# Moving two K copies from VectorE to ScalarE, and cutting an output scaling in two, in a fused attention and token-mixing kernel

## The chip, the cores and the metric

One core of one Trainium2 chip. The metric is the device time of one execution in microseconds (us). "Before" is the kernel before, "changed" is the kernel after the change.

One more measure is used throughout, because end-to-end times scatter by about half a microsecond: the **attention part**, from the start of the first logits matmul (qT by kT) to the end of the span, in the profiled run of each kernel. Both edits lie inside it. And "**lost**" is TensorE time between two matmul starts beyond what that pair of shapes usually takes from start to start in the kernel before.

## The reference, cut to what matters

```python
x = A_x;  xn = _layernorm(x)                       # 2048 x 1024
return x + _A_ref(xn, wq, wk, wv, wo, beta) + _B_ref(xn, w1, b1, w2, b2)
# _A_ref: 32 heads of 32, four segments of 512 rows; per segment s and head:
logits = einsum(qs, ks) * scale + causal_mask
a_dot  = softmax(logits) @ vs
a_mem  = (phi(qs) @ M) / (phi(qs) @ z + 1e-06)     # memory of the earlier segments
o      = g * a_mem + (1 - g) * a_dot
M, z   = M + phi(ks).T @ vs, z + sum(phi(ks))      # phi(t) = t + 1 where t > 0, else exp(t)
# _B_ref: layernorm, two matmuls over the token axis, gelu between (done before the attention part)
```

## The kernel before

The attention part works in 32 units (four heads of one segment each: unit = 8 * segment + group). TensorE's instruction stream is made by hand from three kinds of work: dense projections (q, k, v, output), logits, and the weighting of v by the probabilities. Four PSUM banks hold logits, two hold weighted sums, two hold projections, so a bank that is not evicted in time stops TensorE (the 0.319 us lost at 483.91 and 0.326 us at 503.18, in the table below, are such stops).

```python
def q_job(self, u):            # q of unit u, projected in unit u-2
    def end(b):
        fw.op("act", lambda e: e.activation(self.qT[k][:], self.bank(b), ACT.Copy), ...)

def k_job(self, u):            # K: only for u < 16; from unit 16 K is read from DRAM
    def end(b):
        fw.op("dve", lambda e: e.tensor_copy(self.kT[k][:], self.bank(b)), ...)

def logits(self, u, step):     # four or eight matmuls, then one exponential, then the causal masks
    ...
    fw.op("act", ... ACT.Exp ...)
    for v, kb, _ in blocks:
        fw.op("pool", lambda e: e.affine_select(d, d, ...), ...)

def weigh(self, u, part):      # parts 0, 1, 2; banks 4, 5, 4
    ...                        # reads the masked probabilities, writes bank b
    fw.op("dve", lambda e: e.tensor_tensor(dst, src, eps, op=ALU.add), ..., writes=[self.R_ost[o][part]])

def combine(self, u):          # runs on VectorE between the dense matmuls of the next unit
    def products():            # weighted sums times 1/denominator and gate, 128 x 1024
        fw.op("dve", lambda e: e.tensor_tensor(self.prod[:], ost[:, :, 0:D_HEAD],
              rec.unsqueeze(2).to_broadcast([P, 32, D_HEAD]), op=ALU.mult), ...)
    def add():                 # the memory half plus the softmax half -> o_s
        ...
    return [scales, products, add]

# in attention(), unit u:  logits(u,0) ... weigh(u-1,0), weigh(u-1,1), weigh(u-1,2) ... logits(u,1) ...
```

In the profile `ost` is the eviction of the weighted sums, `kT` the copy of K, `prod` the scaling, `o_s` the sum of both outputs, `fin` the eviction of the output projection, `pT` the exponential (ScalarE) or the mask (POOL, which is GpSimd).

Of the kernel before, what the change touches and what calls it, by code (L numbers as in the profile page):

```python
# [6 lines left out]
ACT = mybir.ActivationFunctionType  # L7
ALU = mybir.AluOpType
# [7 lines left out]
D_HEAD = 32  # L16
# [3 lines left out]
P = 128  # L20
# [366 lines left out]
class _Kernel:  # L387
# [862 lines left out]
    def q_job(self, u):  # L1250
# [5 lines left out]
                self.exps.append((0, self.qT[k], self.R_qT[k], u))  # L1256
        return self.proj_job(self.wq_ring, u, end)

    def k_job(self, u):
        def end(b):  # L1260
            fw, k = self.fw, u % 3
            fw.op("dve", lambda e: e.tensor_copy(self.kT[k][:], self.bank(b)),  # L1262
                  reads=[self.R_bank[b]], writes=[self.R_kT[k]])
            if u // N_GRP < N_SEG - 1:
                self.exps.append((1, self.kT[k], self.R_kT[k], u))
        return self.proj_job(self.wk_ring, u, end)
# [167 lines left out]
    def combine(self, u):  # L1434

        fw = self.fw
        s, g, o = u // N_GRP, u % N_GRP, u % 2
        ost, R_ost = self.ost[o], self.R_ost[o]
        rec, R_rec = self.srec[:, o, :], self.R_srec[o]
        os, R_os = self.o_s[o], self.R_os[o]  # L1440

        def scales_first():
            v = ost[:].rearrange("p (q k r) x -> p q k r x", q=4, k=2)
            rv = rec[:, 0:16].rearrange("p (q r) -> p q r", q=4)
            fw.op("dve", lambda e: e.reciprocal(rv, v[:, :, 0, :, D_HEAD]), reads=R_ost, writes=[R_rec])
            fw.op("dve", lambda e: e.tensor_tensor(rv, rv, self.gate[:, g, None, 0, :].to_broadcast([P, 4, 4]),
                                                   op=ALU.mult), reads=[R_rec, self.R_gate], writes=[R_rec])

        def products_first():
            v = ost[:].rearrange("p (q k r) x -> p q k r x", q=4, k=2)  # L1450
            rv = rec[:, 0:16].rearrange("p (q r) -> p q r", q=4)
            fw.op("dve", lambda e: e.tensor_tensor(os[:].rearrange("p q (r d) -> p q r d", d=D_HEAD),
                                                   v[:, :, 0, :, 0:D_HEAD],
                                                   rv.unsqueeze(3).to_broadcast([P, 4, 4, D_HEAD]), op=ALU.mult),
                  reads=R_ost + [R_rec], writes=[R_os])

        def scales():
            sums = ost[:, :, D_HEAD].rearrange("p (q a) -> p q a", q=4)
            rv = rec.rearrange("p (q a) -> p q a", q=4)
            g8 = self.gate[:, g, :, :].rearrange("p k r -> p (k r)")[:, None, :].to_broadcast([P, 4, 8])  # L1460
            fw.op("dve", lambda e: e.reciprocal(rv, sums), reads=R_ost, writes=[R_rec])
            fw.op("dve", lambda e: e.tensor_tensor(rv, rv, g8, op=ALU.mult), reads=[R_rec, self.R_gate], writes=[R_rec])

        def products():
            fw.op("dve", lambda e: e.tensor_tensor(self.prod[:], ost[:, :, 0:D_HEAD],  # L1465
                                                   rec.unsqueeze(2).to_broadcast([P, 32, D_HEAD]), op=ALU.mult),
                  reads=R_ost + [R_rec], writes=[self.R_prod])

        def add():
            pv = self.prod[:].rearrange("p (q k r) d -> p q k (r d)", q=4, k=2)  # L1470
            fw.op("dve", lambda e: e.tensor_tensor(os[:], pv[:, :, 0, :], pv[:, :, 1, :], op=ALU.add),
                  reads=[self.R_prod], writes=[R_os])

        if s == 0:
            return [scales_first, products_first]
        return [scales, products, add]

    def o_transpose_dma(self, u):
# [199 lines left out]
```

## Time and profile before

| | kernel before |
|---|---|
| median of six runs beside the change (lowest, highest) | 652.36 us (652.19, 652.78) |
| span of the profiled run | 650.55 us |
| TensorE / VectorE / ScalarE / GpSimd busy | 99% / 67% / 43% / 24% |
| first logits matmul, attention part | 387.50 us, 263.05 us |
| lost in front of a weighting, waiting for `ost` behind a K copy | 0.319 us at 483.91, 0.326 us at 503.18 |
| lost in front of a weighting, waiting for a mask | 0.154 us at 547.74, 0.154 us at 577.70 |

TensorE is the bound, and it is nearly full. A change that does not touch TensorE's work can win only what TensorE loses in waits. A matmul of 512 columns is recorded with 0.38 us although the next one starts 0.215 us after it, so recorded matmuls overlap; this is why the waits are taken from starts.

### The profile page before, as it was taken

What the parts mean: (1) busy time and instruction counts of PE and PEld (TensorE: products, weight loads), DVE (VectorE), ACT (ScalarE), POOL (GpSimd) and SP (SyncE); (2) the same over time, 40 slices, a digit from 0 to 9 for tenths busy, and PEclk for the clock granted to TensorE, in tenths of its full rate; (3) what the DMA queues carried; (4) which work ended last, traced back from release to release, by engine and by line L of the source; (5) the groups of instructions that cost most, each with busy time, mean ns of one, the idle gap of its engine ahead of it and who ended that gap; (6) DMA issues with size and microseconds to landing.
All of it is one profiled execution on the core that took longest, in us unless ns stands there. A gap on an engine that the chain in (4) does not pass through costs nothing.

```text
span 650.5 us, 11182 instructions
## 1 busy us (share of the span) xinstructions
PE 645.9 (99%) x4611; PEld 303.6 (47%) x4611; DVE 433.7 (67%) x808; ACT 281.4 (43%) x305; POOL 154.2 (24%) x179
## 2 busy tenths in 40 slices
PE   9999999999999999999999999999999999999998
PEld 3444444444444444444444444444544454445544
DVE  6975676665555664744638325767887888777896
ACT  7543232232210000111101047778767778889770
POOL 2500000000011220220202203343334444554440
PEclk9999999999999999999999999999999999999999
DMA  9804233242498947538262957979654677435434
GB/s 303 216 0 130 65 107 88 64 116 79 127 261 193 238 120 210 157 102 231 79 208 96 263 130 177 184 168 227 134 135 98 155 165 139 112 98 128 105 94 139
DMA packets 190123, 95.00 MB, mean 146 GB/s; under 512 B 108664, under 2 KB 176248, under 8 KB 190072
## 3 DMA queue, kind: packets, MB, share of 16 engines
q1 hardware_dynamic: 189928, 94.25, 57.2%
q8 instruction: 36, 0.59, 0.4%
q14 instruction: 15, 0.12, 0.1%
q10 hardware_dynamic: 144, 0.03, 0.0%
HBM read 69.23 MB, written 11.53 MB: 124 GB/s over the span
## 4 chain that ended last, share of the span: by engine, by line
PE 94%; DVE 3%; ACT 2%; issue 1%; DMA 0%; POOL 0%; DVEq 0%
PE ps_all L199 94%; ACT pT L1364 1%; DVE prod L1465 1%; DVE ln_st L587 1%; DMA xin<-in_A_x_dram 0%; DVE h L627 0%; DVE ost L1418 0%; POOL ln_rs L611 0%; DVE mtmp L1230 0%; DVE kT L1262 0%; DVE fin L1307 0%; DVE mtmp L1228 0%; ACT qT L1253 0%; ACT vA L1293 0%; DVE ln_mv L590 0%
## 5 line engine op out<-in xcount | busy, mean ns | idle before, releaser
L1364 ACT ACTIVATE pT<-ps_all 128x2048 bf16<-128x2048 f32 x80 | 150.2, 1877 | 47.4 <-PE ps_all L199 46.9
L1368 POOL TENSOR_SCALAR_AFFINE_SELECT pT<-pT 128x512 bf16<-128x512 bf16 x128 | 105.6, 843 | 160.7 <-ACT pT L1364 160.7
L689 DVE TENSOR_TENSOR part<-ps_all,part 128x512 f32<-128x512 f32 x84 | 57.7, 690 | 108.2 <-PE ps_all L199 87.8
L1075 POOL TENSOR_TENSOR part<-part,stg 128x512 f32<-128x512 f32 x24 | 33.0, 1404 | 285.1 <-DVE part L689 285.1
L199 PE MATMUL ps_all<-wv,xnT 128*128 128x512 bf16 x256 | 68.5, 380 | 0.4 <-ACT qT L1253 0.2
L746 ACT ACTIVATE g<-part,b1c 128x512 f16<-128x512 f32 x36 | 26.0, 722 | 98.8 <-DVE part L689 98.8
L199 PE MATMUL ps_all<-xnT,wq 128*128 128x512 bf16 x256 | 66.4, 380 | 0.0
L199 PE MATMUL ps_all<-wo,oT 128*128 128x512 bf16 (+2 forms) x272 | 63.8, 367 | 0.0
L694 ACT ACTIVATE part<-ps_all 128x512 f32<-128x512 f32 x24 | 14.0, 596 | 101.1 <-PE ps_all L199 67.1
L1418 DVE TENSOR_TENSOR ost<-ps_all,eps 128x396 bf16<-128x396 f32 (+1 forms) x72 | 37.2, 522 | 28.5 <-PE ps_all L199 27.8
L199 PEld LDWEIGHTS ps_all<-vA,pT 128*128 128x128 bf16 x1280 | 45.7, 96 | 20.4 <-DVE ost L1418 1.7
L199 PE MATMUL ps_all<-g,sum 128*128 128x512 f16 x224 | 51.0, 379 | 0.0
L199 PE MATMUL ps_all<-g,w2s 128*128 128x512 f16 x224 | 51.0, 379 | 0.0
L199 PE MATMUL ps_all<-gT,sum 128*128 128x512 f16 x224 | 50.3, 379 | 0.0
L199 PE MATMUL ps_all<-vA,pT 128*128 128x33 bf16 x1280 | 48.5, 177 | 0.3 <-DVE ost L1418 0.3
L199 PE MATMUL ps_all<-h,sum 128*128 128x512 f16 x192 | 45.2, 379 | 0.0
L199 PE MATMUL ps_all<-h,w1s 128*128 128x512 f16 x192 | 44.9, 379 | 0.0
L199 PE MATMUL ps_all<-hT,sum 128*128 128x512 f16 x192 | 43.6, 379 | 0.0
L199 PEld LDWEIGHTS ps_all<-wo,oT 128*128 128x128 bf16 x272 | 23.9, 98 | 24.4 <-issue 3.7
L199 PEld LDWEIGHTS ps_all<-xnT,wq 128*128 128x128 bf16 x256 | 22.6, 97 | 25.4 <-issue 5.3
L199 PEld LDWEIGHTS ps_all<-g,sum 128*128 128x128 f16 x224 | 21.9, 98 | 26.4
L199 PEld LDWEIGHTS ps_all<-g,w2s 128*128 128x128 bf16 x224 | 21.9, 98 | 26.4
(118 smaller groups left out, 875.1 us busy)
## 6 DMA issues: line engine op xcount, KB each, us to landing
w2s<-in_B_w_dram SPq DMA_DIRECT2D x8, 1792.0 KB, 9.5
w1s<-in_B_w_dram SPq DMA_DIRECT2D x12, 1024.0 KB, 5.6
wq<-in_A_wq_dram SPq DMA_DIRECT2D x32, 256.0 KB, 3.3
xs<-in_A_x_dram SPq DMA_DIRECT2D x24, 256.0 KB, 3.4
stg<-in_A_x_dram SPq DMA_DIRECT2D x16, 256.0 KB, 2.9
out_dram<-stg SPq DMA_DIRECT2D x16, 256.0 KB, 3.9
wk<-in_A_wk_dram SPq DMA_DIRECT2D x16, 256.0 KB, 3.6
fin<-out_dram SPq DMA_DIRECT2D x16, 256.0 KB, 3.2
```

What stands on the lines that cost most here:

```text
L199: ins = self.nc.tensor.matmul(*args, **kwargs)
L587: fw.op("dve", lambda e: e.bn_stats(st[:, 6 * h:6 * h + 6], src[:, 512 * h:512 * h + 512]), reads=[self.R_xin[c]], writes=[R])
L689: self.fw.op("dve", lambda e: e.tensor_tensor(self.tmp[dst][:], self.bank(b), self.tmp[src][:], op=ALU.add), reads=[self.R_bank[b], self.R ...
L694: self.fw.op("act", lambda e: e.activation(self.tmp[dst][:], self.bank(b), ACT.Copy), reads=[self.R_bank[b]], writes=[self.R_tmp[dst]])
L746: self.fw.op("act", lambda e: e.activation(self.gB[f % 2][half][:, f // 2, :], src, ACT.Gelu_apprx_tanh, bias=self.b1c[:, f:f + 1], scale= ...
L1075: fw.op("pool", lambda e: e.tensor_tensor(self.tmp[t][:], self.tmp[t][:], self.stg[k][:, 512 * half:512 * half + 512], op=ALU.add), reads= ...
L1364: fw.op("act", lambda e: e.activation(dst, src, ACT.Exp, scale=SCALE), reads=self.R_bank[0:4], writes=[R[v % 2][kb] for v, kb, _ in blocks ...
L1368: fw.op("pool", lambda e: e.affine_select(d, d, pattern=[[0, 4], [1, P]], compare_op=ALU.is_ge, fill=0.0, base=0, channel_multiplier=-1), ...
L1418: fw.op("dve", lambda e: e.tensor_tensor(dst, src, eps, op=ALU.add), reads=[self.R_bank[b], self.R_eps], writes=[self.R_ost[o][part]])
L1465: fw.op("dve", lambda e: e.tensor_tensor(self.prod[:], ost[:, :, 0:D_HEAD], rec.unsqueeze(2).to_broadcast([P, 32, D_HEAD]), op=ALU.mult), ...
```

## The change

Its intent: in two units the K copy stands in VectorE's queue right before the eviction that TensorE waits for, so it goes to ScalarE. And in later units the long scaling holds up a causal mask on GpSimd that TensorE waits for (the one at 546.09 takes 1.50 us where the median mask takes 0.637), so in seven of them it is cut in two, to let the mask in between.

```diff
+    K_BY_ACT = (13, 15)
     def k_job(self, u):
         def end(b):
-            fw.op("dve", lambda e: e.tensor_copy(self.kT[k][:], self.bank(b)), ...)
+            if u in self.K_BY_ACT:
+                fw.op("act", lambda e: e.activation(self.kT[k][:], self.bank(b), ACT.Copy), ...)
+            else:
+                fw.op("dve", lambda e: e.tensor_copy(self.kT[k][:], self.bank(b)), ...)
 ...
         def products():
-            fw.op("dve", lambda e: e.tensor_tensor(self.prod[:], ost[:, :, 0:D_HEAD], ...
+            parts = ((0, 16), (16, 32)) if u >= 18 and u % 2 == 0 else ((0, 32),)
+            for a0, a1 in parts:
+                fw.op("dve", lambda e: e.tensor_tensor(self.prod[:, a0:a1], ost[:, a0:a1, 0:D_HEAD], ...
```

More of the change, by code (lines that the diff above doesn't have):

```diff
@@ L1261, in end @@
             fw, k = self.fw, u % 3
-            fw.op("dve", lambda e: e.tensor_copy(self.kT[k][:], self.bank(b)),
-                  reads=[self.R_bank[b]], writes=[self.R_kT[k]])
+            if u in self.K_BY_ACT:
+                fw.op("act", lambda e: e.activation(self.kT[k][:], self.bank(b), ACT.Copy),
+                      reads=[self.R_bank[b]], writes=[self.R_kT[k]])
+            else:
+                fw.op("dve", lambda e: e.tensor_copy(self.kT[k][:], self.bank(b)),
+                      reads=[self.R_bank[b]], writes=[self.R_kT[k]])
             if u // N_GRP < N_SEG - 1:
@@ L1464, in products @@
         def products():
-            fw.op("dve", lambda e: e.tensor_tensor(self.prod[:], ost[:, :, 0:D_HEAD],
-                                                   rec.unsqueeze(2).to_broadcast([P, 32, D_HEAD]), op=ALU.mult),
-                  reads=R_ost + [R_rec], writes=[self.R_prod])
+            parts = ((0, 16), (16, 32)) if u >= 18 and u % 2 == 0 else ((0, 32),)
+            for a0, a1 in parts:
+                fw.op("dve", lambda e: e.tensor_tensor(self.prod[:, a0:a1], ost[:, a0:a1, 0:D_HEAD],
+                                                       rec[:, a0:a1].unsqueeze(2).to_broadcast([P, a1 - a0, D_HEAD]),
+                                                       op=ALU.mult), reads=R_ost + [R_rec], writes=[self.R_prod])
         def add():
```

## The prediction

> **What bounds the kernel now.** I began with the page: busy time by engine, then the chain of work that ended last.
>
> ```profile
> PE 645.9 (99%) x4611; PEld 303.6 (47%) x4611; DVE 433.7 (67%) x808; ACT 281.4 (43%) x305; POOL 154.2 (24%) x179
> PE 94%; DVE 3%; ACT 2%; issue 1%; DMA 0%; POOL 0%; DVEq 0%
> ```
>
> TensorE is busy for 99% of a 650.5 us span and makes 94% of the chain. Neither edited part touches TensorE's own work, so the change can only give back time in which TensorE waits for someone. The chain in order of time shows where, in the attention part:
>
> ```profile
> 482.09 0.69 DVE mtmp L1230
> 482.78 0.60 DVE kT L1262
> 483.38 0.49 DVE ost L1418
> 483.87 0.05 issue
> 483.91 11.86 PE ps_all L199 x127
> ...
> 502.05 0.60 DVE kT L1262
> 502.65 0.49 DVE ost L1418
> 503.14 0.05 issue
> 503.18 42.96 PE ps_all L199 x485
> ```
>
> Columns are start, length, what. Twice the chain leaves TensorE for a burst on VectorE that ends with the K copy out of PSUM (kT, L1262) and the eviction of the weighted sums (ost, L1418), for which TensorE waits. K for unit u is projected in unit u-2, and the 32 groups of 512-column logits number the units, so these two copies are K of units 13 and 15, exactly the pair that the change names. No later unit has one (from unit 16 K comes from DRAM), and the earlier ones are not on the chain.
>
> How long TensorE really stands still is not the bracketed idle time, because matmuls overlap and their ends are modelled. I use starts. Eight 512-column matmuls in a row show as 1.90 us while one shows 0.38, so the pitch is (1.90 - 0.38)/7 = 0.217 us (start to start 0.215).
>
> ```profile
> 483.17 0.59 PE L199 MATMUL ps_all<-wv,xnT 128*128 128x512 bf16 x2
> 483.91 0.24 PE L199 MATMUL ps_all<-vA,pT 128*128 128x33 bf16 x3 [0.16 <-DVE ost L1418]
> ...
> 502.00 1.02 PE L199 MATMUL ps_all<-wv,xnT 128*128 128x512 bf16 x4
> 503.18 0.29 PE L199 MATMUL ps_all<-vA,pT 128*128 128x33 bf16 x5 [0.16 <-DVE ost L1418]
> ```
>
> Two matmuls from 483.17 are through at 483.60, the next starts at 483.91: 0.31 us lost. Four from 502.00 are through at 502.86, the next starts at 503.18: 0.32 us lost.
>
> The second edit is for another wait, which the profile does not name. I found it by laying GpSimd's causal masks (affine select, L1368) beside VectorE's scaling (L1465):
>
> ```profile
> 545.88 1.22 DVE L1465 TENSOR_TENSOR prod<-ost,srec 128x1024 bf16<-128x1024 bf16 x1
> 546.09 1.50 POOL L1368 TENSOR_SCALAR_AFFINE_SELECT pT<-pT 128x512 bf16<-128x512 bf16 x1 [2.77 <-ACT pT L1364]
> 547.13 0.74 DVE L1471 TENSOR_TENSOR o_s<-prod 128x512 bf16<-128x512 bf16 x1
> ...
> 547.37 0.38 PE L199 MATMUL ps_all<-wv,xnT 128*128 128x512 bf16 x1
> 547.74 0.25 PE L199 MATMUL ps_all<-vA,pT 128*128 128x33 bf16 x4
> ```
>
> A mask takes 0.637 us (median of the 128); this one takes 1.50 and ends at 547.59, about 0.5 us after the scaling ends at 547.10. The next weighting needs that mask and starts 0.15 us later; TensorE could have started at 547.37 + 0.215 = 547.585, so 0.155 us is lost. The same picture recurs at 577.70 (0.145 lost). In the five other units concerned it isn't there: at 562.84 the mask is only just in time (0.01 lost), at 592, 607, 621 and 635 it ended well before.
>
> [...] The K copies here have a median of 690 ns and the scaling 1218[...]. [...] the q copies out of PSUM here take 592 to 603. [...] the q copies stand between exponentials and no load follows. [...] masks beside the scaling go from 0.637 to 1.5 us, the scaling itself from 1.218 to 1.655 where a mask came first, and each side gets its turn when one instruction of the other ends (o_s takes 0.740 instead of 0.417 at 547.13, +0.32).
>
> **The change part by part.**
>
> K to ScalarE. VectorE loses 2 x 0.69 us. In both bursts its ost eviction starts 0.60 earlier (the start-to-start step from the K copy): 482.70 instead of 483.30, ending 483.26; with the 0.05 us of issue TensorE may go at 483.31, before the 483.60 at which it is free. In the other unit, 502.52 + 0.05 against 502.86. The stalls go entirely, with some 0.29 us to spare: 0.31 + 0.32 = **0.63 us** gained. ScalarE gains 2 x 0.6 us. Its surroundings:
>
> ```profile
> 479.12 0.60 ACT L1253 ACTIVATE qT<-ps_all 128x512 bf16<-128x512 f32 x1
> 481.19 1.88 ACT L1364 ACTIVATE pT<-ps_all 128x2048 bf16<-128x2048 f32 x1 [1.47 <-PE ps_all L199]
> 485.60 1.88 ACT L1364 ACTIVATE pT<-ps_all 128x2048 bf16<-128x2048 f32 x1 [1.00 <-PE ps_all L199]
> ...
> 504.43 1.88 ACT L1364 ACTIVATE pT<-ps_all 128x2048 bf16<-128x2048 f32 x1 [0.57 <-PE ps_all L199]
> ```
>
> K's last matmul ends at 480.82 (478.93 + 1.89), so the copy runs from about 480.85 to 481.45 in the 1.47 us idle stretch. It pushes the exponential that was to start at 481.19 back by 0.2 us. Before the next exponential ScalarE idles 1.00 us, in the second unit 0.57; TensorE arriving 0.32 earlier and the 0.2 delay use up 0.52. It fits, the second time just barely. Nothing for it on the path.
>
> The scaling in halves. It acts in seven units (outputs 18, 20 ... 30). One half should take 692 ns, as the first segment's 512-element scaling does (691 to 692 undisturbed). The second waits for the first through the semaphore of the shared tile, starting 0.03 us after it as dependent neighbours do. Undisturbed the pair takes 0.69 + 0.03 + 0.69 = 1.41 us, 0.19 more than 1.22. In return the mask gets its turn at half time: first half 545.88 to 546.57, mask through at about 547.07 instead of 547.59, in time for TensorE. But the mask's turn now falls into the second half (+0.32, as it did into o_s), and the second mask's turn still falls into o_s. VectorE is then behind by 0.19 + 0.32 = 0.5 us: ost would end at 548.95 + 0.51 = 549.46 and free TensorE at 549.51. Without the first stall TensorE wants that bank at 549.60 - 0.155 = 549.445. About 0.07 of the gain is lost again: 0.085 us kept in this unit, 0.075 at 577. In the others VectorE idles about 0.4 us before that eviction and the slack at 564.70 is 0.7, so the delay is swallowed; 0.01 is gained. Sum **0.17 us**.
>
> Total 0.63 + 0.17 = 0.80 us: 652.3 - 0.8 = 651.5.
>
> **The rivals.** (1) ScalarE takes over as the wait: the pushed exponential delays the next or holds PSUM. For it: at 504 the margin is 0.05. Against it: ScalarE is 43% busy and idles 1.47 before the place. It could take back 0.1 to 0.3: 651.6 to 651.8. (2) The mask does not get in between the halves, or VectorE's lag costs more at the eviction than the mask saves. For it: the margin is negative by my own sum. Then the second edit is worth 0 to -0.3 and the time is 651.6 to 652.0. (3) The mask wait goes and VectorE isn't late, because the masks collide less than I add up: 0.30 instead of 0.17, 651.35. (4) Something later absorbs it all: stalls behind ScalarE at 555.73 and 561.75, or the DMA transpose of unit 30's output, which lands at 639.88 while TensorE wants it near 640.5. Against it: those ScalarE chains start from TensorE's own logits and move with it. It would leave 652.0 to 652.3.
>
> **Range and chances.** The three runs before lie between 652.26 and 652.78. Most weight is on 651.3 to 651.9, with (4) and run scatter above and (3) below: range 651.0 to 652.2. A 2% change would be 13 us; all waits of TensorE that I find in the attention part sum to about 4 us, and no added instruction is longer than 0.7 us. So within 2%: 0.99.
>
> **What would show it.** Chain: no kT and no ost near 483 and 503; ScalarE kT of 0.59 to 0.60 us there; the weighting starts 0.215 after its neighbour. Scaling: 14 halves of 0.69 to about 1.0; the masks near 546 and 576 about 1.0 instead of 1.5; the weighting at 547 without a gap, a new one of under 0.1 before the part at 549. I am wrong if ScalarE's kT delays logits, if a mask still waits for both halves, or if TensorE's gain by 505 is not 0.6 us.

The sum came to 0.63 us for the K copies and 0.17 us for the halves, 0.80 us in all, and each term is worked out from times in the trace of the kernel before. The time of a K copy on ScalarE is that of its 32 q copies (591 to 603 ns, median 592), the time of a half that of its 512-element scalings in the first segment (691 to 692 ns undisturbed). That the long scaling itself can be halved at that price was the estimate; the changed kernel's undisturbed halves took 684 to 685 ns. As to table loads on ScalarE, the trace has two, at 0.81 and 263.92 us, and the changed kernel's has two, at 0.81 and 264.23 us: all lie before the attention part, so the copies added none.

## The result, and the profile after

| | before | changed |
|---|---|---|
| median of six runs (lowest, highest) | 652.36 us (652.19, 652.78) | 651.73 us (651.32, 652.03) |
| first logits matmul | 387.50 us | 388.06 us |
| attention part | 263.05 us | 262.23 us |

The ratio is 0.9989 with a 95% interval from 0.9976 to 1.0002: within 2%, and an interval that just reaches 1. Ratios are computed as the mean time of one kernel's fast runs over that of the other's in the same rounds, so they are not quite the ratio of the medians that are quoted. By medians the change saves 0.63 us; the attention part is 0.82 us shorter. The first logits matmul of each kernel is the start of these lines of the tile view (instructions that read kT; shortest, median and longest in ns, first and last start, shapes), the kernel before first:

```profile
L199 PE MATMUL ps_all<-qT,kT x512: 214/304/385, 387.5 to 630.9; 32*128 32x512 bf16 x43, 32*128 32x384 bf16 x43, 32*128 32x256 bf16 x43, 32*128 32x128 bf16 x42
```

and the changed kernel:

```profile
L199 PE MATMUL ps_all<-qT,kT x512: 214/305/385, 388.1 to 630.6; 32*128 32x512 bf16 x43, 32*128 32x384 bf16 x43, 32*128 32x256 bf16 x43, 32*128 32x128 bf16 x42
```

The changed kernel's profiled run entered the attention part 0.56 us later and left it earlier. That later start lies before any edited instruction, and a repeat of the same kernel (e3 below) started at 387.50 like the kernel before, so it is scatter of the run. It also fell on a run of 652.03 us, the slowest of the six.

The page of the changed kernel, busy times by engine and shares of the chain that ended last:

```profile
PE 645.2 (99%) x4611; PEld 303.6 (47%) x4611; DVE 435.0 (67%) x813; ACT 282.3 (43%) x307; POOL 152.3 (23%) x179
PE 92%; DMA 3%; ACT 2%; DVE 2%; SPq 1%; issue 0%; ACTq 0%; DVEq 0%
```

ScalarE has two more instructions; VectorE has five more (seven second halves less two K copies) and 1.3 us more work, although it gave two copies away. No load tells that the kernel got faster. The chain's shares are not to be compared here: its early stretch now runs through DMA transfers of weights before the attention part. What matters is the chain in order of time (start, length, what):

```profile
390.44 155.61 PE ps_all L199 x1696
546.04 0.03 issue
```

It does not leave TensorE between 390 and 546 us any more; before, it left twice, for stretches on VectorE that ended near 483 and 503. What TensorE won there is seen by busy time in equal stretches (stretch, its length, then busy time and count by engine, clock, DMA). The kernel before:

```profile
480.00:486.00 6.00, 5.84 (x77) 3.00 (x76) 5.41 (x11) 3.81 (x5) 2.21 (x3) 1.00 0.53 131
500.00:506.00 6.00, 5.84 (x77) 3.19 (x77) 5.34 (x14) 4.97 (x5) 1.48 (x2) 1.00 0.54 97
```

and the changed kernel:

```profile
480.00:486.00 6.00, 6.00 (x79) 3.17 (x78) 5.24 (x11) 4.34 (x7) 2.77 (x3) 1.00 0.58 149
500.00:506.00 6.00, 6.00 (x79) 3.33 (x78) 5.08 (x13) 5.57 (x6) 1.70 (x2) 1.00 0.52 116
```

TensorE (first pair) goes from 5.84 to 6.00 us of 6, that is, no gap is left. ScalarE, the fourth, is at 5.57 of 6 in the second stretch: little room there. The matmuls of the two places in the timeline of the changed kernel:

```profile
483.72 0.59 PE L199 MATMUL ps_all<-wv,xnT 128*128 128x512 bf16 x2
484.15 0.41 PE L199 MATMUL ps_all<-vA,pT 128*128 128x33 bf16 x10
...
502.22 1.02 PE L199 MATMUL ps_all<-wv,xnT 128*128 128x512 bf16 x4
503.08 0.38 PE L199 MATMUL ps_all<-vA,pT 128*128 128x33 bf16 x9
```

The weighting follows two wide matmuls by 0.43 us and four by 0.86 us, exactly their pitch of 0.215 us. Both waits are gone. ScalarE at the first place and before the exponential of the second:

```profile
481.41 0.60 ACT L1265 ACTIVATE kT<-ps_all 128x512 bf16<-128x512 f32 x1 [1.13 <-PE ps_all L199]
481.90 1.87 ACT L1370 ACTIVATE pT<-ps_all 128x2048 bf16<-128x2048 f32 x1
485.82 1.88 ACT L1370 ACTIVATE pT<-ps_all 128x2048 bf16<-128x2048 f32 x1 [0.53 <-PE ps_all L199]
```

The copy takes 0.60 us in ScalarE's idle time and pushes the exponential back by 0.15 us (it would have started at 481.19 plus the run's later start of 0.56 us). Before the next exponential ScalarE still idles 0.53 us; it keeps 0.09 us at the second place.

The second edit, around the mask at the first of its two places, VectorE, GpSimd and then TensorE in the changed kernel:

```profile
545.79 1.72 DVE L1473 TENSOR_TENSOR prod<-ost,srec 128x512 bf16<-128x512 bf16 x2
545.99 0.98 POOL L1374 TENSOR_SCALAR_AFFINE_SELECT pT<-pT 128x512 bf16<-128x512 bf16 x1 [2.78 <-ACT pT L1370]
548.80 0.55 DVE L1424 TENSOR_TENSOR ost<-ps_all,eps 128x396 bf16<-128x396 f32 x1
...
547.27 0.38 PE L199 MATMUL ps_all<-wv,xnT 128*128 128x512 bf16 x1
547.49 0.26 PE L199 MATMUL ps_all<-vA,pT 128*128 128x33 bf16 x4
548.70 0.81 PE L199 MATMUL ps_all<-wv,xnT 128*128 128x512 bf16 x3
549.41 0.24 PE L199 MATMUL ps_all<-vA,pT 128*128 128x33 bf16 x3
```

The mask takes 0.98 us instead of 1.50, and the weighting follows its neighbour by 0.22 us instead of 0.37. The price: the two halves took 0.685 and 1.002 us, VectorE came late to the eviction at 548.80, and three matmuls from 548.70 were through at 549.345, while the next weighting started at 549.41. That is 0.067 us lost anew, and 0.068 us in the same way at 579.29.

The recorded times of both kernels show how masks and VectorE's instructions stretched each other here. From 461 us on, each mask that started during a scaling, a half or the `o_s` after it and was stretched ended 0.49 to 0.50 us after that instruction's end; the median mask takes 0.637 us. In turn, those that VectorE started during a mask ended a nearly fixed time after the mask's end: `o_s` 0.27 to 0.28 us (0.417 undisturbed), a second half 0.54 us (0.685), a whole scaling 1.07 to 1.08 us (1.218). Each of these is 0.14 us less than the instruction takes undisturbed; why, no run here shows.

### The profile page after: what moved, and what is told of

It is laid out like the page before. It is cut to its first block, busy times and chain, and to the rows that moved or that the text cites. A ratio compares the mean times of both kernels' runs of the same rounds, so it can differ in the third digit from the quotient of the medians.

```text
span 650.3 us, 11189 instructions
## 1 busy us (share of the span) xinstructions
PE 645.2 (99%) x4611; PEld 303.6 (47%) x4611; DVE 435.0 (67%) x813; ACT 282.3 (43%) x307; POOL 152.3 (23%) x179
## 4 chain that ended last, share of the span: by engine, by line
PE 92%; DMA 3%; ACT 2%; DVE 2%; SPq 1%; issue 0%; ACTq 0%; DVEq 0%
PE ps_all L199 92%; ACT pT L1370 1%; DMA w2s<-in_B_w_dram 1%; DMA w1early<-in_B_w_dram 1%; SPq L221 1%; DMA pk_part<-part 1%; DVE sum L648 1%; DVE part L689 0%; ACT qT L1253 0%; ACT vA L1299 0%; DVE gT L663 0%; DVE sumk L648 0%; DVE stg L1083 0%; DVE part L1009 0%; DVE kout L994 0%
## 5 line engine op out<-in xcount | busy, mean ns | idle before, releaser
L1374 POOL TENSOR_SCALAR_AFFINE_SELECT pT<-pT 128x512 bf16<-128x512 bf16 x128 | 103.8, 829 | 161.7 <-ACT pT L1370 161.7
L1473 DVE TENSOR_TENSOR prod<-ost,srec 128x1024 bf16<-128x1024 bf16 (+1 forms) x31 | 35.9, 1158 | 0.3
L199 PEld LDWEIGHTS ps_all<-gT,sum 128*128 128x128 f16 x224 | 21.9, 98 | 26.8 <-DVE gT L663 0.6
```

The costliest lines, as they stand in the source:

```text
L199: ins = self.nc.tensor.matmul(*args, **kwargs)
L1374: fw.op("pool", lambda e: e.affine_select(d, d, pattern=[[0, 4], [1, P]], compare_op=ALU.is_ge, fill=0.0, base=0, channel_multiplier=-1), ...
L1473: fw.op("dve", lambda e: e.tensor_tensor(self.prod[:, a0:a1], ost[:, a0:a1, 0:D_HEAD], rec[:, a0:a1].unsqueeze(2).to_broadcast([P, a1 - a0 ...
```

## The experiments

The main theory, called A: TensorE waits for one instruction that stands *behind* another one, an `ost` eviction behind a K copy in VectorE's queue, and a mask behind a whole scaling; the change wins because of the order of these, and each wait is worth what is lost in front of that one weighting. Its rivals, spelled out in the expectations where they are first tested: the gain comes of a lighter VectorE, the more relief the better; halving the scaling is good everywhere; TensorE waits for what the profile names and not for the mask; and, later, that the latency of the wait itself is what can be won.

All kernels gave correct results. Each "e" kernel was timed in five runs, beside nine of the kernel before on the same chip.

| run | median us (before) | ratio, 95% interval | attention part us, against 263.05 |
|---|---|---|---|
| changed | 651.73 (652.36) | 0.9989, 0.9976 to 1.0002 | 262.23, -0.82 |
| e1_k_only | 651.55 (652.31) | 0.9988, 0.9975 to 1.0000 | 262.40, -0.65 |
| e2_halves_only | 652.18 (652.31) | 0.9997, 0.9984 to 1.0009 | 262.92, -0.13 |
| e3_both_again | 651.42 (652.31) | 0.9986, 0.9973 to 1.0000 | 262.24, -0.81 |
| e4_k_behind_ost | 651.53 (652.31) | 0.9990, 0.9977 to 1.0002 | 262.41, -0.64 |
| e5_all_k_act | 651.81 (652.39) | 0.9992, 0.9979 to 1.0004 | 262.54, -0.51 |
| e6_odd_halves_too | 651.50 (652.19) | 0.9989, 0.9977 to 1.0002 | 262.40, -0.65 |
| e7_masks_swapped | 654.05 (652.39) | 1.0025, 1.0013 to 1.0038 | 264.62, +1.57 |
| e8_add_behind_ost | 651.25 (652.39) | 0.9983, 0.9970 to 0.9995 | 262.00, -1.05 |
| e9_q_by_vector_too | 651.11 (652.39) | 0.9981, 0.9967 to 0.9994 | 261.81, -1.24 |
| e10_all_and_wait_order | 650.41 (652.19) | 0.9973, 0.9961 to 0.9986 | 261.31, -1.74 |
| e11_wait_order_alone | 651.98 (652.19) | 0.9995, 0.9982 to 1.0009 | 262.76, -0.29 |

The medians of two sets of the same changed kernel differ by 0.31 us (651.73 and 651.42), its attention parts by 0.01 us. So tenths are read from the attention part and the lost times at each place, and the medians only confirm the direction. Each attention part is one profiled run.

### e1_k_only and e2_halves_only: each part by itself

```diff
# e1: the K part alone
-            parts = ((0, 16), (16, 32)) if u >= 18 and u % 2 == 0 else ((0, 32),)
+            parts = ((0, 32),)
# e2: the halves alone
-    K_BY_ACT = (13, 15)
+    K_BY_ACT = ()
```

> Only the first part: K of units 13 and 15 leaves PSUM by ScalarE, the scaling stays whole. Theory A (the two parts are independent; TensorE waited for the ost eviction because the K copy stood before it in VectorE's queue): the waits near 483 and 503 (0.32 and 0.33 us lost between matmul starts) are gone, the two mask waits near 547 and 577 stay at 0.15 each; 0.63 us less than before, ratio about 0.9990. Rival B (the gain of the whole change comes from the masks and the scaling): under 0.2 us less.

Measured: -0.65 us. The `ost` waits are gone, the mask waits stay at 0.154 and 0.155 us.

> Only the second part: the scaling of outputs 18 to 30 in halves, K stays on VectorE. Theory A: the waits near 483 and 503 stay (0.32 and 0.33), the mask waits near 547 and 577 go (0.15 each), new waits of 0.07 each for the ost eviction appear about 1.8 us later; net 0.17 us less than before, which is inside the run scatter, so the trace decides. Rival B: most of the 0.6 to 0.7 us of the whole change.

Measured: -0.13 us. The `ost` waits stay (0.322 and 0.326 us), both mask waits are gone, and 0.067 and 0.062 us are lost at the evictions that follow. The parts add up: 0.65 + 0.13 = 0.78 us against 0.81 and 0.82 together. Four fifths of the gain is the two K copies.

### e3_both_again: the changed kernel once more

No edit.

> The changed kernel once more, same chip and rounds as the two parts. Theory A: 0.80 us less than before in the attention part, ratio 0.9988, with up to 0.5 us of scatter from run to run that lies before the attention part begins (the profiled run of the changed kernel began it 0.56 us later than that of before). If the scatter is not in the early part but the change costs something there, the start of the first logits is again some 0.5 us later than before's 387.5.

Measured: -0.81 us, with the first logits at 387.50. The changed kernel's late start in its own profile was scatter, and the attention part repeats.

### e4_k_behind_ost: the K copy stays on VectorE, but behind the eviction

On the kernel before:

```diff
+    K_LATE, held = (13, 15), None
     def k_job(self, u):
-        def end(b):
+        def copy(b):
             ...
+        def end(b):
+            if u in self.K_LATE:
+                self.held = lambda: copy(b)
+            else:
+                copy(b)
 ...
                 self.weigh(u - 1, 0)
+                if self.held:
+                    self.held()
+                    self.held = None
```

> K of units 13 and 15 stays on VectorE but is queued behind the first ost eviction instead of before it; scaling whole. No work is taken off VectorE, and kT and its PSUM bank come free later than before. Theory A (the order in VectorE's queue is the whole matter): the waits near 483 and 503 go as in the ScalarE version, 0.63 us less than before. Rival C (what helps is less VectorE work, or kT and its bank free earlier): the waits stay or grow, no gain.

The timeline of this kernel at the first place:

```profile
483.02 0.56 DVE L1427 TENSOR_TENSOR ost<-ps_all,eps 128x396 bf16<-128x396 f32 x1
483.50 0.68 DVE L1265 CAST kT<-ps_all 128x512 bf16<-128x512 f32 x1
483.49 0.59 PE L199 MATMUL ps_all<-wv,xnT 128*128 128x512 bf16 x2
483.92 0.26 PE L199 MATMUL ps_all<-vA,pT 128*128 128x33 bf16 x4
```

The eviction comes first, the copy after it, and the weighting follows its two matmuls by 0.43 us: nothing lost. The gain is 0.64 us, that of e1, without one instruction taken off VectorE. So the relief of VectorE is not the cause; the place in its queue is.

### e5_all_k_act: all sixteen K copies on ScalarE, scaling whole

```diff
-    K_BY_ACT = (13, 15)
+    K_BY_ACT = tuple(range(16))
```

> K of all 16 units that project it in the attention part leaves by ScalarE, scaling whole. Theory A (only the two places where VectorE's queue made TensorE wait count): the same as with 13 and 15 alone, 0.65 us less than before in the attention part, 0 to 0.3 of it lost again where the K copy pushes an exponential that TensorE needs. Rival D (relieving VectorE is what pays): some 0.3 us for each further copy, 3 us or more in all.

Measured: -0.51 us, 0.14 us worse than two copies. The only new loss lies at the start of the attention part: at 390.06 us, 0.368 us instead of 0.221. There ScalarE's K copy at 387.64 (0.60 us) stands before an exponential, which starts at 388.13 instead of 387.94 and ends at 390.00, and TensorE's next logits start 0.06 us after that end. Twelve of the other copies win nothing, and one, at 377.28, lies before the attention part. More relief does not pay, and moving work to the engine with more idle time costs where that engine is itself waited for.

### e6_odd_halves_too: halves in the odd units too

```diff
-            parts = ((0, 16), (16, 32)) if u >= 18 and u % 2 == 0 else ((0, 32),)
+            parts = ((0, 16), (16, 32)) if u >= 18 else ((0, 32),)
```

> The changed kernel with the scaling of the odd outputs from 19 on in halves too. Theory A (halves help only where a mask that TensorE needs next waits for the scaling; in these units four masks in a row are ready or VectorE is behind anyway): nothing gained, attention part within 0.1 us of the changed kernel or longer by up to 0.3 through later VectorE work. Rival H (half-size instructions are better as such): a further 0.1 to 0.2 us less.

Measured: -0.65 us, that is, 0.16 us longer than the changed kernel. One new wait of 0.149 us accounts for it, at 613.51, before a q projection: VectorE, behind by the longer pair, had two `fin` evictions queued one after the other (1.27 us from 612.69), and a projection bank came free late. Cutting costs VectorE time (two undisturbed halves of 0.685 us are 0.15 us more than a whole scaling of 1.218) and was good here only where a mask was late.

### e7_masks_swapped: the needed mask second

This one is slower on purpose. In units 19 and 23, the ones with the two mask waits, the two masks after the second exponential run in the other order, on the kernel before:

```diff
-        for v, kb, _ in blocks:
+        for v, kb, _ in (blocks[::-1] if u in (19, 23) and step == 1 else blocks):
```

> The kernel before, with the two masks of the units 19 and 23 in the other order, so that the mask which the next weighting needs is GpSimd's second instead of its first. Theory A (TensorE waits near 547 and 577 for that mask, although the profile says only issue): the weighting starts 0.15 us after the second mask's end, near 548.5 instead of 547.74, 0.8 us lost more in each of the two, ratio 1.0024. Rival E (the gap is instruction issue or something else): unchanged, ratio 1.000.

GpSimd and TensorE in this kernel's timeline:

```profile
546.30 1.51 POOL L1368 TENSOR_SCALAR_AFFINE_SELECT pT<-pT 128x512 bf16<-128x512 bf16 x1 [2.78 <-ACT pT L1364]
547.76 0.81 POOL L1368 TENSOR_SCALAR_AFFINE_SELECT pT<-pT 128x512 bf16<-128x512 bf16 x1
...
547.58 0.38 PE L199 MATMUL ps_all<-wv,xnT 128*128 128x512 bf16 x1
548.72 0.25 PE L199 MATMUL ps_all<-vA,pT 128*128 128x33 bf16 x4 [0.76 <-DVE fin L1307]
```

The needed mask now ends at 547.76 + 0.81 = 548.57, and the weighting starts 0.15 us after that. The loss at each place rose from 0.154 to 0.927 us; 2 x 0.773 = 1.55 us, and the attention part is 1.57 us longer. The weighting does wait for that mask. The profile puts this wait down to `fin`, an eviction on VectorE; in the kernel before it named nothing at all. By time alone `fin` is a rival: it ended at 548.68, after the mask. But the weighting reads nothing of `fin` in the code, and the trace holds a separate wait for the mask's semaphore in front of the weighting, which starts 0.04 us after the mask's end, as in the kernel before; the steps from there to the matmul are the same too (0.11 us), so the later `fin` added nothing. A named releaser is a hint, and moving the suspected instruction is the test.

### e8_add_behind_ost: the remaining lateness of VectorE

On the changed kernel, the `o_s` sum of units 14, 18 and 22, and with it the DMA transpose of its result, goes behind the eviction that comes after it:

```diff
+    ADD_LATE, held = (14, 18, 22), None
 ...
                 self.weigh(u - 1, 0)
+                if self.held:
+                    self.held()
+                    self.held = None
 ...
+                if u - 1 in self.ADD_LATE:
+                    steps[-1] = lambda late=steps[-1]: setattr(self, "held", late)
```

> The changed kernel, and the sum of both outputs (o_s) of units 14, 18 and 22 is queued behind the first ost eviction of the next even unit instead of before it. Theory A (the new waits of 0.07 us near 549 and 579 and the old one of 0.09 near 519 are VectorE's queue, which the halves made 0.5 us longer): all three go, 0.22 us less than the changed kernel, about 1.0 us less than before in the attention part, ratio 0.9984. Rival: the waits stay because the eviction waits for something else, or move to the later output transposes.

Measured: -1.05 us. The waits at 519 (0.087), 549 (0.067) and 579 (0.068), 0.22 us together, are gone, and the attention part is 0.23 us shorter than the changed kernel's. It is e4's lesson again: the halves' extra work on VectorE costs TensorE only where an eviction that it waits for stands behind it.

### e9_q_by_vector_too: two q copies to VectorE

On e8, for units 22 and 26, where an exponential waits behind a q copy on ScalarE:

```diff
+            if u in (22, 26):
+                fw.op("dve", lambda e: e.tensor_copy(self.qT[k][:], self.bank(b)), ...)
+            else:
                 fw.op("act", lambda e: e.activation(self.qT[k][:], self.bank(b), ACT.Copy), ...)
```

> The same, and q of units 22 and 26 leaves PSUM by VectorE instead of ScalarE, because TensorE waits 0.25 us near 555.6 and 0.16 near 585.4 for the bank that ScalarE empties only after an exponential. Theory A (what counts is whose queue the eviction stands in): VectorE has finished o_s at 554.6 and 584.5, so q is out some 0.2 us earlier and both waits shrink to under 0.05; 0.35 to 0.4 us less than the run without it, ratio to before 0.9978. It would be wrong if VectorE's later fin and ost then make TensorE wait.

Measured: -1.24 us, 0.19 us more. The waits near 555 and 585 fell from 0.251 to 0.050 and from 0.161 to 0, together 0.36 us, but about 0.08 us was lost anew at each of 567.02 and 596.15. The logits there wait for the same things as before, yet with q now from VectorE the kernel's helper emits the waits in the other order. That raised a question that the prediction had not asked: does the *order* in which a matmul's waits are listed cost time?

### e10_all_and_wait_order: the late semaphore's wait emitted first, on top of e9

```diff
-        for t in need.values():
+        toks = list(need.values())
+        if es.name == "pe":
+            rank = {"pool": 1, "dve": 2, "act": 3}
+            if self.late:
+                rank[self.late] = 4
+            toks.sort(key=lambda t: -rank.get(t.key, 0) if isinstance(t.key, str) else 0)
+        for t in toks:
             es.wait_tok(t)
 ...
+        fw.late = "pool" if part == 0 else None     # around the weighting's matmuls
```

No wait is dropped by this edit: the trace of e11, which has it alone, shows 131 separate wait instructions on TensorE, as the kernel before does. The wait emitted first ends up on the matmul's own weight load, the others are separate instructions ahead of it (in the kernel before, at the mask near 547, a separate wait starts at 547.64 and the weight load with the other wait at 547.71).

> The previous candidate (K of 13 and 15 by ScalarE, halves, late sum, q of 22 and 26 by VectorE) with the waits of each TensorE instruction put in another order: the semaphore that comes last in practice (ScalarE; in the first part of a weighting GpSimd) is the one on the instruction itself, the others are waited for before it. No wait is dropped. Theory F (a TensorE instruction starts 0.05 us after its releaser when the late semaphore is its own, 0.14 when a further, long satisfied wait follows; seen when the move of q turned the order round at 567 and 596): the waits of 0.09 at 545, 560, 567, 575, 590, 596, 604, 618 and the like go or lose 0.09 each, 1.0 us less in the attention part than without it, 2.2 less than before, ratio 0.9965. Rival G (the 0.09 belong to what the instructions do, not to the order of waits): same time as without it, ratio 0.9981.

Measured: 650.41 us, -1.74 us; -2.2 had been expected. It is the fastest kernel: its 650.27 to 650.85 us lie below every run of the kernel before and of the changed kernel. The waits of about 0.09 us before logits are gone, but others of 0.16 us remain (560.29, 589.47, 617.96). I had expected these to shrink as well, so the theory needed a run of its own.

### e11_wait_order_alone: the same edit on the kernel before

> The kernel before with that order of waits alone. Theory F: the mask waits near 547 and 577 shrink from 0.15 to 0.06, those of 0.09 for the exponential near 546, 561, 576, 591, 605 and 619 go, the waits for ScalarE's evictions near 556 and 562 lose 0.09; the two waits for ost near 484 and 503 stay 0.32. 1.1 us less in the attention part than before, ratio 0.9983, so more than the change itself. Rival G: no change, ratio 1.000.

Measured: -0.29 us, where -1.1 had been expected. The mask's wait in this kernel:

```profile
546.87 1.51 POOL L1374 TENSOR_SCALAR_AFFINE_SELECT pT<-pT 128x512 bf16<-128x512 bf16 x1 [2.78 <-ACT pT L1370]
...
548.05 0.38 PE L205 MATMUL ps_all<-wv,xnT 128*128 128x512 bf16 x1
548.43 0.24 PE L205 MATMUL ps_all<-vA,pT 128*128 128x33 bf16 x3
```

The mask ends at 548.38 and the weighting starts 0.05 us later, instead of 0.14 (547.60 to 547.74 before). At logits it is the same: from the exponential's end to the matmul 0.05 us (546.80 to 546.85) instead of 0.14 (546.03 to 546.17). So the latency part of the theory holds: with the late semaphore on the matmul itself the step is 0.09 us shorter. The packed trace, though not the timeline view, shows where. In the kernel before the late semaphore (the mask's) has a wait instruction of its own, of 0.05 us, at 547.64, and the weight load with the satisfied wait follows: 0.12 us from the mask's end to the weight load, 0.03 from there to the matmul. In e11 the satisfied wait ran at 547.33, long before the mask's end, and the two steps are 0.05 and 0.004 us.

But the sum did not hold. At 548.43 TensorE still lost 0.161 us, not 0.06: it had arrived 0.09 us earlier, as the waits of 0.09 us before logits were gone, at a mask that did not come earlier. The mask starts 0.07 us after an exponential on ScalarE in both kernels, and that exponential itself came no earlier: it is TensorE that moved up on it, from 0.14 to 0.05 us behind its end. Beside the scaling the mask takes 1.50 and 1.51 us. At 591 a wait of 0.092 and one of 0.071 us became a single one of 0.163.

The fixed order also costs something that the theory had not foreseen: before an output projection, at 466.12 (465.23 in e10), 0.092 us is lost that the kernel before does not lose. The last two separate waits in front of that matmul run 0.15 us later against the matmuls before it than they do in the kernel before; why, no run here was made to show. Here a shortened latency was kept only where what TensorE waited for next moved with TensorE: of the 1.1 us expected, 0.29.

## Why the prediction was right

The predicted 651.5 us stand against 651.73 and, repeated, 651.42; the predicted gain of 0.80 us against 0.82 and 0.81 us in the attention part.

- **K to ScalarE, 0.63 us.** Right in mechanism and size. e1 gave 0.65. e4 shows that the eviction's place in the queue is the cause, since the copy may stay on VectorE.
- **ScalarE has room, at 504 just barely.** Right: 0.09 us of idle time were left before that exponential where 0.05 had been worked out, and 0.53 against 0.48 at 485. The push was 0.15 us against 0.2. e5 shows that this margin is not everywhere.
- **The halves, 0.17 us.** Right, with a repaid part of the size named: new waits of 0.067 and 0.068 us against 0.07. Alone they gave 0.13 us; on top of the K part 0.16 and 0.17. One reading was off: the loss at 577.70 was 0.154 us, not 0.145, which moves the sum by 0.01. The two halves took 0.685 and 1.002 us against 0.69 and 0.69 + 0.32.
- **The mask is what the weighting waits for.** Argued from start times in the prediction, shown by e7.
- **Rivals.** (1), ScalarE as the new wait, did not come about. (2) and (3) bracketed the repaid part, and the middle was right. (4), a later wait that absorbs the gain, did not come about in the attention part.

What the prediction did not see: it took the 0.15 us from the end of the mask to the weighting as given. e11 shows that 0.09 us of it is the order of that matmul's waits. And it did not say that end-to-end runs begin the attention part at times up to 0.9 us apart (from 387.30 to 388.19 in these runs), which is as large as the gain; its range allowed for it without naming it.

What stays open: where the scatter before the attention part comes from, which no run here was made for; and why the steps of a separate wait take what they take (0.09 us in all more), of which the runs show the sizes only.

## What to carry to other kernels

Where one engine is the bound and almost full (TensorE here, 99% busy), look for the few instructions that it waits for and at what stands in front of them in their engine's queue: reordering alone (e4, 0.64 us) won as much as moving work to another engine (e1, 0.65 us), and a further reordering (e8) another 0.23 us, while moving more of it (e5) lost 0.14 us again and cutting more of it (e6) 0.16 us. Test a suspected wait by making its releaser late, as the releaser named in the profile may be another (e7 names `fin`, while the start followed the mask's end by 0.15 us). And expect that a wait removed may be partly taken over by the next one: in e11 a wait of 0.092 us and one of 0.071 us became one of 0.163 us.
